# Queries and keys of the last batch, one row to a partition instead of eight, and the keys' block copy moved from ScalarE to VectorE

## The chip, the cores and the metric

The kernel runs on one core of one Trainium2 chip. Its time is the device time of one execution in microseconds, and the figure that counts is the median over runs. Before the change it is 291.07 us (8 runs, 290.84 to 291.77). A core has TensorE (PE in the profile; PEld is its weight load), VectorE (DVE), ScalarE (ACT), GpSimd (POOL, here Pool) and SyncE (SP), each with its own in-order instruction queue. All meet through semaphores. SyncE here only issues DMAs; Pool issues some too.

## What is computed

Chunked attention with a short context and eight memory keys, and behind it a mixing layer: two Fourier transforms, a normalisation and a two-layer network.

```python
B, H, S, D = 4, 8, 768, 64                 # batch, heads, rows, head width
for c in range(24):                        # chunks of 32 query rows
    # keys: 8 memory keys, then rows 32c-16 .. 32c+40 inside 0..768
    scores = q_c @ concat(mem_k, k_ctx).T / sqrt(D)
    out_c  = softmax(scores) @ concat(mem_v, v_ctx)
x = out.transpose(0, 2, 1, 3).reshape(B, S, 512)
u = x + real(fft(fft(x, axis=1), axis=2))
un = (u - mean(u)) / sqrt(var(u) + 1e-6)   # over the 512 columns
result = u + relu(un @ w_ch1) @ w_ch2      # 512 -> 2048 -> 512
```

## The kernel before, in words

**Attention.** Work goes by head pairs: `n` = 0 to 15, four pairs a batch, so the last batch (batch 3) has n = 12 to 15. A pair's two heads lie on partitions 0 to 63 and 64 to 127, head width down. Queries are needed as `qT` (128 x 768), keys as `kTb`: 12 blocks of 128 columns, block t serving 64 query rows. Columns 32 to 39 of a block hold the memory keys (`e_mkT`, VectorE), columns 40 to 127 the 88 context keys; neighbouring blocks overlap. Per pair there are two groups g of six blocks: `e_scores` makes 12 matmuls (six blocks, two heads) into the PSUM tile `sc`, `e_exp` takes the exponential on ScalarE (two instructions), `e_values` makes 24 matmuls into `xa` (`v` carries a column of ones that gives the sum), and `e_norm` divides on VectorE and writes into `xsb`. `sc` and `xa` exist once, `qT`, `kTb` and `kU` twice, `qs` and `ks` three times, `va` four times, the query transposes' target slot `qT` being freed by the second group's scores.

**How q and k become transposed.** For batches 0 to 2 (n < `TURNED * HP` = 12) a Pool DMA brings eight consecutive rows to each of 96 partitions (`e_load_qk`, L347), TensorE transposes them in 16 pieces (`turn`, L374), and ScalarE (VectorE in batch 0) copies them into natural order (`e_qT`, `e_kT`). For batch 3 Pool loads the same eight rows a partition, the two heads' columns side by side (L343, one DMA a head); a DMA transpose issued by SyncE turns them (`e_flip_q` L379, `e_flip_k` L382). Its result has the rows in the order (j, p), where row = 8p + j. `e_scores` (L431, L432) undoes that order for the queries by reading 8 runs of 8 and writing 8 x 8 scattered columns in PSUM, and `e_kT` (L410, ScalarE) for the keys, from the staging tile `kU` into `kTb`, 128 x 1056 elements. `kU` has zero margins for keys outside 0 to 767; Pool sets both `kU` tiles to zero at the start (L851).

**Mixing.** Per batch: row transforms (`zy`, `pq`, `ff` on VectorE, split in a high and a low half `hi`, `lo`, then PE matmuls `ps`), PSUM read out by ScalarE (`up`) and VectorE (`e_rest`), column transforms (PE, `pm`, into the PSUM banks `acc`, freed by VectorE's `e_sum` and `e_sum_back`), statistics, `un` on ScalarE, and the two network layers (`ph`, with ScalarE's `hT`, and `pc`, with VectorE's `osb`). For batches 1 to 3 SyncE's DMA transposes turn `un` into `unT` (L711).

**What sets the order.** A planner (`Plan`) gets every step with an engine, a cost, its predecessors and the slots that it takes and gives, runs a list schedule in planned time, and writes the instructions out in that order; the `ph` and `pc` blocks are fillers that it puts where PE would be idle. The order on every queue therefore depends on the planned costs. The steps of batch 3 are made in `attention` (L873 to L878): the two transposes as SP steps of 1.2 us that land 5 us later, the block copy as an ACT step of 2.05 us.

Of the kernel before, what the change touches and what calls it, by code (L numbers as in the profile page):

```python
# [11 lines left out]
BF16 = mybir.dt.bfloat16  # L12
# [5 lines left out]
LEFT = 16  # L18
RIGHT = 8
NMEM = 8  # L20
BIGM = 800.0
MEM0 = 32
# [9 lines left out]
def strided(src, off, dims):  # L32
    return bass.AP(tensor=src.tensor, offset=src.offset + off,
                   ap=[list(src.ap[0])] + [list(d) for d in dims])
# [143 lines left out]
def kernel(  # L178
# [11 lines left out]
    nc = tc.nc  # L190
    B, H, S, D = q.shape
    DM = out.shape[2]
    DFF = moe_w_ch1.shape[1]
    P = 128
    NST = S // P
    NDT = DM // P
    NHT = DFF // P
    NT = S // 64
    RB = 8
    QP = S // RB  # L200
    KP = QP + 4
    KOFF = LEFT // RB
# [8 lines left out]
    spool = ctx.enter_context(tc.tile_pool(name="stage", bufs=1))  # L211
    apool = ctx.enter_context(tc.tile_pool(name="attn", bufs=1))
# [20 lines left out]
        assert False  # L233

    NS = 3
    qs = [spool.tile([QP, 2, RB * D], BF16, name=f"qs{i}") for i in range(NS)]
    ks = [spool.tile([KP, 2, RB * D], BF16, name=f"ks{i}") for i in range(NS)]
    NV = 4
    va = [spool.tile([P, 2, NT, 66], FP32, name=f"va{i}") for i in range(NV)]
    NKT = 2  # L240
    KR, KS, NKU = 16, 128, 2
    kU = [spool.tile([P, RB, KS], BF16, name=f"kU{i}") for i in range(NKU)]
    kTb = [spool.tile([P, NT, P], BF16, name=f"kTb{i}") for i in range(NKT)]

    TURNED = 3
    cp_q = "p h j d -> p h (j d)"
    HP = H // 2
# [4 lines left out]
    add = plan.add  # L252
# [19 lines left out]
    ident_b = cpool.tile([P, P], BF16)  # L272
    turn_b = cpool.tile([KP, KP], BF16)
# [64 lines left out]
    def e_load_qk(n, i):  # L338
        b, pr = seq[n]
        src, dst = ((q, qs), (k, ks))[i]  # L340
        if b >= TURNED:
            for hh in range(2):
                nc.gpsimd.dma_start(  # L343
                    dst[n % NS][0:QP].rearrange("p h (j d) -> p (h j) d", d=D)[:, hh::2],
                    src[b, 2 * pr + hh].rearrange("(p j) d -> p j d", j=RB))
            return
        nc.gpsimd.dma_start(dst[n % NS][0:QP],  # L347
                            src[b, 2 * pr:2 * pr + 2].rearrange("h (p j) d -> p h (j d)", j=RB))
# [21 lines left out]
    def turn(out_, src, eye):  # L370
        w = eye.shape[1]
        for j in range(RB):
            for hh in range(2):
                nc.tensor.transpose(out_[64 * hh:64 * hh + 64, j * w:(j + 1) * w],  # L374
                                    src[:, hh, j * D:(j + 1) * D], eye)

    def e_flip_q(n):
        qT_of[n] = qT = apool.tile([P, RB, QP], BF16, tag="qT", bufs=2, name="qT")
        nc.sync.dma_start_transpose(qT, qs[n % NS].rearrange("p h c -> p (h c)"))  # L379

    def e_flip_k(n):
        nc.sync.dma_start_transpose(kU[n % NKU][:, :, KR:KR + QP],  # L382
                                    ks[n % NS][0:QP].rearrange("p h c -> p (h c)"))

    def e_turn_q(n):
        tr_of[n] = trq = aps.tile([P, S], BF16, tag="tr", bufs=1, name="trq")
        turn(trq, qs[n % NS], ident_b[0:QP, 0:QP])

    def e_qT(n):
        qT_of[n] = qT = apool.tile([P, S], BF16, tag="qT", bufs=2, name="qT")  # L390
# [3 lines left out]
    def e_turn_k(n):  # L394
        if n < HP:
            trk = bank("acc", [P, RB * KP], BF16, "trk")
        else:
            trk = aps.tile([P, RB * KP], BF16, tag="tr", bufs=1, name="trk")
        tr_of[n, 1] = trk
        turn(trk, ks[n % NS], turn_b)  # L400

    def e_mkT(n):
        b, pr = seq[n]
# [3 lines left out]

    def e_kT(n, eng=None):
        if n >= TURNED * HP:
            nc.scalar.copy(  # L410
                strided(kTb[n % NKT], MEM0 + NMEM, [[P, NT], [RB, 11], [1, RB]]),
                strided(kU[n % NKU], KR - KOFF, [[64 // RB, NT], [1, 11], [KS, RB]]))
            return
        trk = tr_of.pop((n, 1))
        (eng or nc.scalar.copy)(
            strided(kTb[n % NKT], MEM0 + NMEM, [[P, NT], [RB, 11], [1, RB]]),
            strided(trk, 0, [[64 // RB, NT], [1, 11], [KP, RB]]))
        if n < HP:
            let_go(trk)

    def e_scores(n, g):
        qT, kT = qT_of[n], kTb[n % NKT]
        sc_of[n, g] = sc = aps.tile([P, 2, 8, 64], FP32, tag="sc", bufs=1, name="sc")
        for t6 in range(6):
            t = 6 * g + t6
            for hh in range(2):
                r0 = 64 * hh
                if n < TURNED * HP:
                    own, to = qT[r0:r0 + 64, ts(t, 64)], sc[:, hh, t6, :]
                else:  # L430
                    own = strided(qT[r0:r0 + 64], t * 64 // RB, [[QP, RB], [1, 64 // RB]])  # L431
                    to = strided(sc[:, hh, t6, :], 0, [[1, RB], [RB, 64 // RB]])  # L432
                nc.tensor.matmul(to, kT[r0:r0 + 64, t, :], own, start=True, stop=True,  # L433
                                 tile_position=(r0, 0))

    def e_exp(n, g):
# [416 lines left out]
    def attention(n):  # L853
        nonlocal t_gate
        b, pr = seq[n]
        first = b == 0
        lq, lk = [add("POOL", 1.6 if b >= TURNED else 0.9, lambda i=i: e_load_qk(n, i),
                      take=(("qs", "ks")[i],), moved=3.1 if b >= TURNED else 1.2, grain=0.032 if b >= TURNED else 0.1, late=LATE if b else 0.0,
                      behind=t_gate if n == HP else t_xr[b - 2] if n == TURNED * HP else t_ck.get(n - 1),
                      rank={0: -4 + i, 1: -1.2 + 0.1 * i, 2: 10 + 0.1 * i}.get(n)) for i in range(2)]  # L860
        lv = add("SP", 2.5, lambda: e_load_v(n), [t_ones[n] if n < NV else None],
                 behind=t_x2.get(b - 2),
                 take=("va",), moved=2.6, grain=0.031, head=0.4, late=(0.0, 4.0, LATE, LATE)[b])
        t_lv[n] = lv
        t_ck[n] = lk
        if n == HP - 1:
            def e_gate():
                nc.gpsimd.tensor_copy(gate[64:65], va[n % NV][64:65, 1, NT - 1, 0:1])

            t_gate = add("POOL", 0.1, e_gate, [lv])  # L870
        mk = t_mk[n] = add("DVE", 0.2, lambda: e_mkT(n), [t_mkT, t_kTz[n % NKT], t_mk.get(n - 1)],
                           take=("kTb",))
        if b >= TURNED:  # L873
            eq = add("SP", 1.2, lambda: e_flip_q(n), [lq], take=("qT",), give=("qs",),
                     late=5.0, loose=True, behind=t_flip[0])
            t_flip[0] = tk = add("SP", 1.2, lambda: e_flip_k(n), [lk, t_uz], take=("kU",),
                                 give=("ks",), late=5.0, loose=True, behind=eq)
            ek = add("ACT", 2.05, lambda: e_kT(n), [tk, mk], give=("kU",))  # L878
        else:
            tq = add("PE", 0.40, lambda: e_turn_q(n), [lq, t_idb], take=("tr",), give=("qs",))  # L880
            dve = ("DVE", nc.vector.tensor_copy) if n < HP else ("ACT", None)
            eq = add("ACT", 0.80, lambda: e_qT(n), [tq], take=("qT",), give=("tr",),
                     rank=SINES - 0.5 if n == 0 else None)
            ktag = "acc" if first else "tr"
            tk = add("PE", 0.43, lambda: e_turn_k(n), [lk, t_idb, t_kz if n == 0 else t_kzs],
                     take=(ktag,), give=("ks",))
            ek = add(dve[0], 1.25 if dve[1] else 1.04, lambda: e_kT(n, dve[1]), [tk, mk],
                     give=(ktag,))
        for g in range(2):
            s_ = add("PE", 0.32, lambda g=g: e_scores(n, g), [eq, ek], take=("sc",),  # L890
                     give=("qT", "kTb") if g == 1 else ())
            t_sc[n, g] = s_
            t_exp[n, g] = x_ = add("ACT", 1.12, lambda g=g: e_exp(n, g),
                     [s_, t_masks, t_after.get(n)], take=("e1",), give=("sc",))
            tag = "mlp" if first and g == 1 else "xa"
            v_ = add("PE", 0.85, lambda g=g: e_values(n, g), [x_, lv, t_low[n % NV]], take=(tag,),
                     rank=len(plan.tasks) + (50 if (n, g) == (2, 1) else 25) if first else None,
                     give=("e1", "va") if g == 1 else ("e1",))
            take = ("xsb",) if g == 0 and n % HP == 0 else ()
            t_norm[n, g] = add("DVE", 0.78, lambda g=g: e_norm(n, g),  # L900
                               [v_, t_norm[n - n % HP, 0] if (n % HP, g) != (0, 0) else None],
                               take=take,
                               give=(tag,))
        return x_
# [284 lines left out]
```

The softmax here doesn't subtract the row's maximum and nothing guards it: scores larger than these inputs give would overflow.

## Time and profile before

| | before |
|---|---|
| median of 8 runs | 291.07 us |
| profiled execution | 291.56 us, of which span 289.9 us |
| granted TensorE clock over the span | 0.999 |
| PE busy | 273.2 us (94%) |
| ScalarE busy | 167.5 us (58%) |
| VectorE busy | 166.0 us (57%) |
| Pool busy | 65.2 us (22%) |
| PE busy, 127 to 172 us (batch 3's attention, batch 2's transforms) | 45.0 of 45 us |
| VectorE, ScalarE busy, 127 to 172 us | 32.1 and 30.5 us |
| PE, VectorE, ScalarE busy, 214 to 286 us (two-layer network alone) | 71.9, 9.3 and 24.7 of 72 us |

The page of a profile gives the busy time of each engine, the span in 40 slices (a digit is the busy share in tenths, 9 is 90% or more) and the clock in the same slices:

```profile
PE   1588989999999999999999999999999999999994
DVE  7866998862239876958675884985672012012011
ACT  5976545788777687846796466525660721712700
POOL 8853894330201083441001002010020000000000
PEclk9999999999999999999999999999999999999999
```

PE is close to full from the sixth slice on, and the clock is full throughout; slices 18 to 24 (123 to 174 us) are where batch 3's attention runs. Matmuls are pipelined, so a matmul's own duration (some 200 to 400 ns here) overlaps the next one; what a block costs is read from the chain of waits, which follows the work that ended last back from the end and puts blocks end to end. PE's busy digits therefore say only that it did not wait, not that it runs at its best.

### The profile page before, as it was taken

Reading aid. Unit: us, or ns where it says so; the run is one execution under the profiler, and the core shown is the slowest. Engines: PE = TensorE matmul, PEld = TensorE weight load, DVE = VectorE, ACT = ScalarE, POOL = GpSimd, SP = SyncE. Lnnn points to the kernel's source line nnn. Section 1 sums busy time; section 2 is a strip of 40 time slices with the busy share of each in tenths; the row PEclk is TensorE's granted clock in tenths of the full one; section 3 lists DMA queues with packets and bytes.
Section 4 is the critical chain, followed back from the end, with each engine's and each line's share of the span. In section 5 each row is a group of like instructions: output and inputs, shape, how many; then the busy total and the mean of one; then the engine's idle time right before and its main releaser. Section 6 shows DMA issues by size and latency. Waiting matters only on the chain.

```text
span 289.9 us, 7127 instructions
## 1 busy us (share of the span) xinstructions
PE 273.2 (94%) x2932; PEld 170.6 (59%) x2932; DVE 166.0 (57%) x345; ACT 167.5 (58%) x290; POOL 65.2 (22%) x115
## 2 busy tenths in 40 slices
PE   1588989999999999999999999999999999999994
PEld 1465678865665767556676656566654545545541
DVE  7866998862239876958675884985672012012011
ACT  5976545788777687846796466525660721712700
POOL 8853894330201083441001002010020000000000
PEclk9999999999999999999999999999999999999999
DMA  6999999999997999999997047675142504004204
GB/s 106 200 171 162 207 159 205 203 196 196 194 184 222 141 220 164 143 149 247 183 153 200 3 111 144 171 124 180 20 85 84 105 3 126 20 36 108 39 36 109
DMA packets 115968, 39.92 MB, mean 138 GB/s; under 512 B 104544, under 2 KB 111200, under 8 KB 115936
## 3 DMA queue, kind: packets, MB, share of 16 engines
q1 hardware_dynamic: 93744, 23.41, 44.2%
q0 software_dynamic: 21472, 15.21, 33.1%
q10 hardware_dynamic: 720, 0.85, 0.9%
q8 instruction: 23, 0.38, 0.6%
q14 instruction: 9, 0.07, 0.1%
HBM read 37.36 MB, written 13.37 MB: 175 GB/s over the span
## 4 chain that ended last, share of the span: by engine, by line
PE 86%; POOL 5%; DVE 4%; DMA 2%; issue 1%; POOLq 0%
PE pc L756 29%; PE ph L741 29%; PE xa L456 7%; PE ps L528 5%; PE pm L679 5%; PE sc L433 3%; DMA ks<-in_k_dram 2%; PE ps L668 2%; DVE ff L615 2%; PE trk L374 1%; PE trq L374 1%; POOL qs L347 1%; DVE hl L635 1%; DVE xsb L467 1%; PE pm L579 1%
## 5 line engine op out<-in xcount | busy, mean ns | idle before, releaser
L749 ACT ACTIVATE hT<-ph 128x384 f16<-128x384 f32 x128 | 61.9, 491 | 50.6 <-PE ph L741 49.8
L741 PE MATMUL ph<-unT,w_sb 128*128 128x384 f16 x512 | 88.1, 326 | 0.0
L756 PE MATMUL pc<-w_sb,hT 128*128 128x512 f16 x384 | 87.8, 380 | 0.0
L741 PEld LDWEIGHTS <-w_sb 128*128 128x128 f16 x512 | 48.6, 98 | 32.0 <-issue 0.4
L756 PEld LDWEIGHTS <-hT 128*128 128x128 f16 x384 | 35.9, 98 | 41.0 <-issue 0.4
L763 DVE SCALAR_TENSOR_TENSOR osb<-pc,rstd,xsb 128x512 f32<-128x512 f32 x24 | 18.0, 750 | 69.3 <-PE pc L756 64.8
L440 ACT ACTIVATE e<-sc,mbias 128x384 f32<-128x384 f32 x64 | 33.6, 577 | 19.2 <-PE sc L433 18.6
L456 PEld LDWEIGHTS xa<-va,e 128*64 128x64 f32 x672 | 21.9, 137 | 7.2 <-issue 6.2
L456 PE MATMUL xa<-va,e 128*64 128x65 f32 x672 | 25.8, 226 | 0.0
L699 ACT ACTIVATE un<-xsb,mu_s 128x512 f16<-128x512 f32 x24 | 16.9, 719 | 6.6 <-DVE mu_s L694 6.6
L540 ACT CAST up<-ps 128x386 f16<-128x386 f32 x16 | 9.6, 603 | 13.7 <-PE ps L528 11.6
L693 DVE BATCH_NORM_STATS2 st<-xsb 128x6 f32<-128x512 f32 x24 | 16.6, 691 | 0.7
L467 DVE TENSOR_TENSOR xsb<-xa,zs 128x384 f32<-128x384 f32 x28 | 15.6, 558 | 1.0
L466 DVE RECIPROCAL zs<-xa 128x6 f32<-128x6 f32 x28 | 5.3, 190 | 18.1 <-PE xa L456 17.7
L518 DVE TENSOR_TENSOR lo<-ff,hi 128x768 f16<-128x768 f32 x12 | 11.4, 953 | 4.7 <-ACT hi L513 4.7
L545 DVE TENSOR_TENSOR up<-ps,up 128x386 f16<-128x386 f32 x16 | 9.5, 597 | 6.9 <-ACT up L540 6.7
L433 PE MATMUL sc<-qT,kTb 64*128 64x64 bf16 x384 | 12.6, 205 | 0.5 <-ACT e L440 0.5
L374 PE MATMUL trq<-ident_b,qs 96*64 96x96 bf16 x192 | 7.0, 221 | 6.4 <-DMA qs<-in_q_dram 6.4
L433 PEld LDWEIGHTS <-kTb 64*128 64x128 bf16 x384 | 8.5, 100 | 7.3 <-issue 6.1
L513 ACT CAST hi<-ff 128x768 f16<-128x768 f32 x12 | 9.9, 827 | 3.3 <-DVE ff L505 3.0
L685 DVE TENSOR_TENSOR xsb<-pm,xsb 128x512 f32<-128x512 f32 x15 | 10.0, 672 | 3.2 <-PE pm L679 3.2
L571 POOL DMA_DIRECT2D xr<-x_back x3 | 2.3, 779 | 42.1 <-DMA x_back<-x_rows 42.1
(150 smaller groups left out, 356.7 us busy)
## 6 DMA issues: line engine op xcount, KB each, us to landing
va<-in_v_dram SPq DMA_DIRECT2D x32, 220.0 KB
w_sb<-in_moe_w_ch_dram POOLq DMA_DIRECT2D x8, 512.0 KB, 13.5
out_dram<-osb SPq DMA_DIRECT2D x12, 256.0 KB
qs<-in_q_dram POOLq DMA_DIRECT2D x12, 192.0 KB, 6.1
ks<-in_k_dram POOLq DMA_DIRECT2D x12, 192.0 KB, 6.7
x_rows<-xsb POOLq DMA_DIRECT2D x3, 768.0 KB, 5.6
xr<-x_back POOLq DMA_DIRECT2D x3, 768.0 KB, 5.6
out_rows<-osb SPq DMA_DIRECT2D x9, 256.0 KB
```

The lines of the kernel that those rows point to most:

```text
L433: nc.tensor.matmul(to, kT[r0:r0 + 64, t, :], own, start=True, stop=True, tile_position=(r0, 0))
L440: nc.scalar.activation(e1[:, :, :, ts(half, 32)], sc[:, :, 0:6, ts(half, 32)], AFT.Exp, bias=mbias[:, half:half + 1], scale=1.0 / math.sqr ...
L456: nc.tensor.matmul(xa[64 * half:64 * half + 64, st, hh, 0:65], e1[:, hh, t6, :], v1[:, hh, 6 * g + t6, 0:65], start=True, stop=True)
L467: nc.vector.tensor_tensor(xs[b][:, 3 * g:3 * g + 3, 2 * pr * D:(2 * pr + 2) * D] .rearrange("p s (h d) -> p s h d", h=2), xa[:, :, :, 0:D] ...
L528: nc.tensor.matmul(out_[:, sp, :], part[:, ab, sp * 3 + st, c0:c1], tab[:, sp, st, :], start=(st == 0 and i == 0), stop=(st == 2 and i == 1))
L679: nc.tensor.matmul(pm[:, par, :], lhs, rhs[:, par, :], start=(im == 0), stop=(im == 3))
L693: nc.vector.bn_stats(st6, xs[b][:, kt, :])
L699: nc.scalar.activation(un, xs[b][:, kt, :], AFT.Identity, bias=mu_of[b][:, kt, 0:1], scale=-1.0)
L741: nc.tensor.matmul(ph[:, 0:384], w1_sb[:, dt, ts(ht, P)], unT_of[b][:, dt, sh * 384:(sh + 1) * 384], start=(dt == 0), stop=(dt == NDT - 1))
L749: nc.scalar.activation(hT_of[b, sh][:, ht, :], ph[:, 0:384], AFT.Relu, bias=0.0, scale=-1.0)
L756: nc.tensor.matmul(pc_of[b, sh, stl], hT_of[b, sh][:, ht, ts(stl, P)], w2_sb[:, ht, :], start=(ht == 0), stop=(ht == NHT - 1))
L763: nc.vector.scalar_tensor_tensor(osb, pc, rstd_of[b][:, st:st + 1], xs[b][:, st, :], ALU.mult, ALU.add)
```

## The change

For batch 3 only, row 128a + p of a head now goes to partition p (a = 0 to 5), 128 partitions instead of 96, six rows each instead of eight. The DMA transposes, over 768 columns instead of 1024, then give queries and keys in natural order. `qT` is a plain 128 x 768 tile, `e_scores` has one form for all batches, `kU` becomes one run of 768 keys with margins of 16, and the copy into `kTb` reads and writes runs of 88 and is issued on VectorE with a planned cost of 0.6 us instead of 2.05 on ScalarE. `qs` and `ks` get 128 partitions; the older paths use the first 96 or 100 of them.

```diff
-    qs = [spool.tile([QP, 2, RB * D], BF16, name=f"qs{i}") for i in range(NS)]
-    ks = [spool.tile([KP, 2, RB * D], BF16, name=f"ks{i}") for i in range(NS)]
+    qs = [spool.tile([P, 2, RB * D], BF16, name=f"qs{i}") for i in range(NS)]
+    ks = [spool.tile([P, 2, RB * D], BF16, name=f"ks{i}") for i in range(NS)]
...
-    KR, KS, NKU = 16, 128, 2
-    kU = [spool.tile([P, RB, KS], BF16, name=f"kU{i}") for i in range(NKU)]
+    KR, NKU = 16, 2
+    kU = [spool.tile([P, KR + S + KR], BF16, name=f"kU{i}") for i in range(NKU)]
...
             for hh in range(2):
                 nc.gpsimd.dma_start(
-                    dst[n % NS][0:QP].rearrange("p h (j d) -> p (h j) d", d=D)[:, hh::2],
-                    src[b, 2 * pr + hh].rearrange("(p j) d -> p j d", j=RB))
+                    strided(dst[n % NS], hh * D, [[2 * D, NST], [1, D]]),
+                    src[b, 2 * pr + hh].rearrange("(a p) d -> p a d", p=P))
...
     def e_flip_q(n):
-        qT_of[n] = qT = apool.tile([P, RB, QP], BF16, tag="qT", bufs=2, name="qT")
-        nc.sync.dma_start_transpose(qT, qs[n % NS].rearrange("p h c -> p (h c)"))
+        qT_of[n] = qT = apool.tile([P, S], BF16, tag="qT", bufs=2, name="qT")
+        nc.sync.dma_start_transpose(qT.rearrange("p (a s) -> p a s", s=P),
+                                    qs[n % NS].rearrange("p h c -> p (h c)")[:, 0:S])
 
     def e_flip_k(n):
-        nc.sync.dma_start_transpose(kU[n % NKU][:, :, KR:KR + QP],
-                                    ks[n % NS][0:QP].rearrange("p h c -> p (h c)"))
+        nc.sync.dma_start_transpose(kU[n % NKU][:, KR:KR + S].rearrange("p (a s) -> p a s", s=P),
+                                    ks[n % NS].rearrange("p h c -> p (h c)")[:, 0:S])
...
         if n >= TURNED * HP:
-            nc.scalar.copy(
-                strided(kTb[n % NKT], MEM0 + NMEM, [[P, NT], [RB, 11], [1, RB]]),
-                strided(kU[n % NKU], KR - KOFF, [[64 // RB, NT], [1, 11], [KS, RB]]))
+            win = LEFT + 64 + RIGHT
+            nc.vector.tensor_copy(
+                strided(kTb[n % NKT], MEM0 + NMEM, [[P, NT], [1, win]]),
+                strided(kU[n % NKU], KR - LEFT, [[64, NT], [1, win]]))
             return
...
-                if n < TURNED * HP:
-                    own, to = qT[r0:r0 + 64, ts(t, 64)], sc[:, hh, t6, :]
-                else:
-                    own = strided(qT[r0:r0 + 64], t * 64 // RB, [[QP, RB], [1, 64 // RB]])
-                    to = strided(sc[:, hh, t6, :], 0, [[1, RB], [RB, 64 // RB]])
-                nc.tensor.matmul(to, kT[r0:r0 + 64, t, :], own, start=True, stop=True,
+                nc.tensor.matmul(sc[:, hh, t6, :], kT[r0:r0 + 64, t, :],
+                                 qT[r0:r0 + 64, ts(t, 64)], start=True, stop=True,
                                  tile_position=(r0, 0))
...
-            ek = add("ACT", 2.05, lambda: e_kT(n), [tk, mk], give=("kU",))
+            ek = add("DVE", 0.6, lambda: e_kT(n), [tk, mk], give=("kU",))
```

More of the change, by code (lines that the diff above doesn't have):

```diff
@@ L377, in e_flip_q @@
     def e_flip_q(n):
-        qT_of[n] = qT = apool.tile([P, RB, QP], BF16, tag="qT", bufs=2, name="qT")
-        nc.sync.dma_start_transpose(qT, qs[n % NS].rearrange("p h c -> p (h c)"))
+        qT_of[n] = qT = apool.tile([P, S], BF16, tag="qT", bufs=2, name="qT")
+        nc.sync.dma_start_transpose(qT.rearrange("p (a s) -> p a s", s=P),
+                                    qs[n % NS].rearrange("p h c -> p (h c)")[:, 0:S])
     def e_flip_k(n):
-        nc.sync.dma_start_transpose(kU[n % NKU][:, :, KR:KR + QP],
-                                    ks[n % NS][0:QP].rearrange("p h c -> p (h c)"))
+        nc.sync.dma_start_transpose(kU[n % NKU][:, KR:KR + S].rearrange("p (a s) -> p a s", s=P),
+                                    ks[n % NS].rearrange("p h c -> p (h c)")[:, 0:S])
     def e_turn_q(n):
         tr_of[n] = trq = aps.tile([P, S], BF16, tag="tr", bufs=1, name="trq")
-        turn(trq, qs[n % NS], ident_b[0:QP, 0:QP])
+        turn(trq, qs[n % NS][0:QP], ident_b[0:QP, 0:QP])
     def e_qT(n):
@@ L399, in e_turn_k @@
         tr_of[n, 1] = trk
-        turn(trk, ks[n % NS], turn_b)
+        turn(trk, ks[n % NS][0:KP], turn_b)
     def e_mkT(n):
```

## The prediction, made before the changed kernel ran

> **What bounds the kernel now.** I read the waits of TensorE (PE) first: what it waited for, us in total, times, longest.
>
> ```profile
> PE trq L374 <- DMA qs<-in_q_dram: 6.4, 3, 4.8
> ...
> PE trk L374 <- DMA ks<-in_k_dram: 1.2, 2, 0.8
> ...
> PE sc L433 <- ACT e L440: 0.5, 2, 0.3
> ```
>
> All its waits lie in the first 40 us; asked for 110 to 220 us alone the view lists none. So where the last batch's attention runs, the time is the sum of PE's own instructions, and other engines count only if PE comes to wait for them. The chain of waits (start, duration, what) prices these, back to back:
>
> ```profile
> 15.20 0.52 POOL kU L851
> 15.72 0.41 issue
> 16.14 0.95 POOL kU L851
> 17.09 0.58 POOL qs L347
> 17.68 5.96 DMA ks<-in_k_dram
> 23.68 0.55 PE trk L374 x16
> ...
> 121.44 0.28 PE sc L433 x12
> 121.72 4.42 PE pc L756 x20
> ...
> 129.67 1.83 PE pc L756 x8
> 131.50 0.85 PE xa L456 x24
> 132.36 0.44 PE sc L433 x12
> 132.80 2.06 PE ph L741 x12
> ...
> 169.69 1.73 PE pc L756 x8
> ```
>
> Two prices are to be seen. A block of 12 score matmuls costs 0.28 us in batch 2 (121.44) and 0.44 in batch 3 (132.36). And a large block costs 0.1 more after a score or value block (eight `pc` 1.83 after `xa`, 1.73 after `pm`; twelve `ph` 2.06 after scores against 1.95 elsewhere). The first lines show something else: Pool's two `kU` memsets stand ahead of the loads that PE waited for at 23.68.
>
> The rows of the tiles `kU`, `unT` and `sc` (min/median/max ns), then VectorE's copies by form (count, busy us, mean ns):
>
> ```profile
> L382 SPq DMA_TRANSPOSE kU<-ks x4: 1212/1316/2001, 121.6 to 153.8; - x4
> L410 ACT COPY kTb<-kU x4: 2026/2046/2071, 126.8 to 159.5; 128x1056 bf16<-128x1056 bf16 x4
> L711 SPq DMA_TRANSPOSE unT<-un x18: 1188/1214/1436, 116.4 to 215.7; - x18
> L433 PE MATMUL sc<-qT,kTb x144: 190/243/243, 110.4 to 168.5; 64*128 64x64 bf16 x144
> ```
>
> ```profile
> L415 DVE COPY kTb<-trk 128x1056 bf16<-128x1056 bf16 x4 | 5.0, 1254 | 1.7 <-PE trk L374 1.7
> L404 DVE COPY kTb<-mkT 128x96 bf16<-128x96 bf16 x16 | 3.6, 235 | 9.0 <-PE sc L433 8.9
> L553 DVE COPY dn<-up 128x768 f16<-128x768 f16 x4 | 1.4, 362 | 0.1
> ```
>
> **Part by part**
>
> *Scores.* Batch 3 has 4 head pairs (n = 12 to 15) of 2 blocks each. Plain runs are what batch 2 has, same shape: 8 x (0.44 - 0.28) = **-1.28 us**, all on PE.
>
> *Key copy.* ScalarE loses 4 x 2.05 = 8.2 us. PE waits for none of it, so this itself brings nothing. VectorE gains four copies, a form that the trace does not show. Nearest rows: 768 two-byte elements from SBUF take 362 ns, 96 take 178 to 191 when undisturbed, so 0.27 ns an element, and 1056 take **0.44 us**. Upper end 1.25, the row from PSUM. I take 0.44; VectorE is 71% busy from 127 to 172 us, and the four make 1.8 us of its 13 idle.
>
> *The planner's order.* The copy's planned cost falls from 2.05 to 0.6, and the planner lays out all queues anew. The changed program's instruction lists agree with the old up to the values of n = 11 (128.82). Then scores of n = 12 come 2.7 us earlier; those of 13 move behind `ph` and batch 2's even row transforms (`ps`), those of 14 and 15 behind its first column blocks (`pm`). From the last values on it is nearly the old order. PE does the same work, but it goes from a small block to a large one 17 times instead of 15: 2 x 0.1 = **+0.2 us**.
>
> Does PE now wait? I laid the old durations along the new lists from 129.67, each engine in order. The tight places:
> - Scores of 12, PE at 129.67. `kU` landed by 126.8 (ScalarE's copy starts there after waiting), VectorE ends the normalisation ahead of it at 127.83, the copy at 128.3 (129.1 at 1.25): spare 1.4 (0.6). Queued behind this copy is the next normalisation, whose values end only at 131.7.
> - Batch 2's first `ps`: PE 141.9, `lo` done 140.4. Its last `ps`: PE 153.2; `lo`, now behind the copy of 13, 151.5.
> - Third `pm` block: PE 162.8, its bank is read out at 162.1: spare **0.65**, the least.
> - Values of 14: PE 170.75. Their bank is freed by the normalisation of 13, which stands behind all six sums and statistics: 169.95, spare 0.8. The copy of 15 follows at 170.4, scores of 15 at 172.3.
>
> I cost the new order at no wait; each us by which a producer passes its spare is a us lost. On SyncE the transposes of 15 wait for the scores of 13 and go out near 155.5 instead of 152.4, covered until 170; batch 2's `un` transposes behind them are wanted near 187.
>
> *Transposes.* 96 x 1024 becomes 128 x 768: equal bytes. The issue takes 1.2 us at best for `kU` as for 128 x 512 `unT`: no change. Landing: the old key transpose of 12 took 5.2 us (121.56 to 126.8); 7 still fit. I take the old time.
>
> *Loads.* 768 pieces either way: 96 x 8 before, 128 x 6 now, 128 bytes at the destination. What grows shorter is the source's run, from 2048 bytes a partition to 256. The Trainium skill, DMA: Bandwidth & Descriptors, Specifications, speaks against this: under 512 bytes a transfer falls below line rate. The row for these loads is 3.5/7.6/9.3 us from issue to landing. If pieces count, nothing changes. If the rule means the source run and the time doubles, 15.2 us for the queries of 12 (second half issued at 102.65) end at 117.9, and their transpose, now at 114.28, slips 3.6 us with SyncE's queue behind it. Scores of 12 then wait 1.2 us. The old destination pieces are already below 512, so I take the row: 0.
>
> *Shared port.* The skill's SBUF - State Buffer, SBUF: two separate sides, lets a two-port VectorE copy and a Pool instruction exclude each other. Pool issues key loads from 127.34 to 128.95, over the copy of 12. By the rule the copy may end at 128.95 + 0.44 = 129.4, still before 129.67. The trace is mixed: a `mkT` copy took 0.98 us at 31.99 beside a Pool tensor operation, 0.18 at 124.88 beside another. Either way the sum holds.
>
> *Memset.* `kU` shrinks from 1024 to 800 elements. Pool's memset rows: 974 ns for 1024, 423 for 384, so 0.86 ns an element, 2 x 0.19 = 0.39 us earlier loads for n = 3. The end at full effect is -0.39. The other is 0: DMA is saturated there, and Pool's next work waits for values until 26.3. I take **-0.2**.
>
> **Sum:** -1.28 + 0.2 - 0.2 = -1.28, rounded -1.3. The profiled execution took 291.56 (span 289.9 and 1.66 around it): 290.3. It lies 0.5 above the median 291.07, so the median goes to **289.8**.
>
> **Rivals**
> - *B, the new order makes PE wait.* For: spares of 0.65 and 0.8 hang on a VectorE 71% busy, and the old order kept 1.3 at the same two places. Against: laid out with measured durations, none is passed. A wait of about 1 us: 290.8.
> - *C, late key transpose (slower).* Short source runs double the longest landing, 9.3, to 18.6: queries of 12 land at 121.3, their transpose slips 7 us, and the keys', fourth behind it on the same queue, lands at 133.8. Scores of 12, moved forward, wait until 134.3: 4.6 us, so 294.4. It turns the gain into a loss once the key transpose lands after 130.4. For: the skill's rule. Against: equal pieces, the 11.6 us of cover.
> - *E, the scattered order is not what makes scores slow,* so -1.28 goes and 291.1 stays. Against: 190 and 243 ns for one shape in one kernel.
>
> **Numbers.** Forecast 0.68, B 0.16, C 0.10, E 0.06. The forecast's own range is 289.4 (full memset gain, no extra 0.2) to 290.1 (none); with B, E and 0.2 of measurement it becomes 289.2 to 291.6, leaving out C and little more. No change means within 0.2%, 0.58 us, about what a measurement can tell. Faster: 0.66 from the forecast and 0.04 from B. Same: 0.02, 0.07 from B, 0.05 from E. Slower: 0.10 from C, 0.05 from B, 0.01 from E. So 0.70, 0.14, 0.16.
>
> **What would show it.** In the changed profile: score blocks of 0.28 in batch 3; `kTb` copies near 0.44 on VectorE; no PE wait after 110 us; transposes still at 1.2; PE's last values near 178.5 instead of 178.87; `trk` of n = 3 before 23.68. PE waiting for `kTb` near 129.7 would mean C, for VectorE at `pm` or `xa` between 160 and 175 B, scores at 0.44 E.

## The result, and the profile after

| | before | after |
|---|---|---|
| median, both measured in turn | 291.22 us (290.39 to 293.34, 53 runs) | **289.84 us** (289.22 to 291.7, 18 runs) |
| ratio after / before, 95% interval | | **0.9959** [0.9946, 0.9971] |
| profiled execution, span | 291.56, 289.9 us | 291.15, 289.4 us |
| ScalarE, VectorE busy, 127 to 172 us | 30.5 and 32.1 us | 25.1 and 35.8 us |

The ratio makes -1.19 us (-0.84 to -1.57); the medians alone lie 1.38 apart. So the change is faster, and the predicted 289.8 us is met. The profiled pair, though, differs by 0.4 us only, and that has to be explained. First the waits of TensorE (PE) in the changed kernel (what it waited for, us in total, times, longest), whole span:

```profile
PE trq L374 <- DMA qs<-in_q_dram: 6.6, 4, 4.6
PE mps L910 <- DVE mkb L904: 1.8, 1, 1.8
...
PE trk L374 <- DMA ks<-in_k_dram: 0.8, 2, 0.5
```

and the same view asked for 44 to 127 us alone:

```profile
PE trq L374 <- DMA qs<-in_q_dram: 1.2, 2, 0.7
```

The second answer is new: the kernel before waited for nothing after 40 us. From 127 us on PE waits for nothing here either. The chain of waits of the changed kernel (start, duration, what) says where the two late waits are and what followed:

```profile
15.15 0.52 POOL kU L849
15.67 0.18 issue
15.85 0.78 POOL kU L849
16.62 0.57 POOL qs L347
17.20 6.45 DMA ks<-in_k_dram
23.64 0.04 issue
23.69 0.54 PE trk L374 x16
...
54.54 18.81 DMA qs<-in_q_dram
73.34 0.04 issue
73.39 0.53 PE trq L374 x16
...
126.83 0.85 PE xa L454 x24
...
130.36 0.28 PE sc L430 x12
130.64 0.97 PE pc L754 x4
...
179.14 0.85 PE xa L454 x24
...
285.51 0.75 DVE osb L761
```

Three things are to be seen. First, both `kU` memsets are shorter and the loads of n = 3 go out at 17.20 instead of 17.68, yet `trk` starts at 23.69 instead of 23.68: the landing took 6.45 instead of 5.96. Second, batch 1's queries held PE at 73.39 (0.46 us, and 0.71 at 58.06). Third, the scores of batch 3 now cost 0.28 (130.36). The rows of the tiles `sc` (asked for 110 to 260 us, as before), `kU` and `kTb` (min/median/max ns) of the changed kernel:

```profile
L430 PE MATMUL sc<-qT,kTb x144: 190/190/200, 111.1 to 175.9; 64*128 64x64 bf16 x144
L383 SPq DMA_TRANSPOSE kU<-ks x4: 1209/1218/1372, 122.6 to 157.7; - x4
L412 DVE COPY kTb<-kU x4: 425/426/520, 128.4 to 170.5; 128x1056 bf16<-128x1056 bf16 x4
```

To compare kernels across executions I cut PE's chain at three points that exist in all of them: the first large `pm` block (near 47 us), the values of n = 10, second group (the `xa` block near 126 us; before has it at 126.14), and the last `osb` (before 285.89):

```profile
126.14 0.85 PE xa L456 x24
...
285.89 0.75 DVE osb L763
```

The **middle stretch** lies between the first two, the **late stretch** between the last two; batch 3's attention is in the late one. What each kernel is follows below.

| kernel | `pm` at | `xa` at | last `osb` at | middle | late |
|---|---|---|---|---|---|
| before | 47.79 | 126.14 | 285.89 | 78.35 | 159.75 |
| **after** | 47.16 | 126.83 | 285.51 | **79.67** | **158.68** |
| e1 memsets long | 47.05 | 125.41 | 284.09 | 78.36 | 158.68 |
| e2 margins only | 48.16 | 126.52 | 285.20 | 78.36 | 158.68 |
| e3 scattered write | 47.92 | 126.28 | 286.23 | 78.36 | 159.95 |
| e4 read in runs | 47.26 | 125.62 | 284.30 | 78.36 | 158.68 |
| e5 write and read | 48.10 | 126.45 | 286.41 | 78.35 | 159.96 |
| e6 copy on ScalarE | 47.04 | 125.40 | 283.86 | 78.36 | 158.46 |
| e7 longer statistics | 46.38 | 124.73 | 284.40 | 78.35 | 159.67 |
| e8 ten copies | 47.17 | 125.52 | 290.04 | 78.35 | 164.52 |
| e9 old layout, VectorE | 46.80 | 125.15 | 285.11 | 78.35 | 159.96 |
| e10 memsets twice | not in its chain | 126.14 | 284.82 | | 158.68 |
| e11 memsets behind | 47.03 | 125.39 | 284.06 | 78.36 | 158.67 |
| e12 both of e6 and e11 | 46.99 | 125.35 | 283.81 | 78.36 | 158.46 |

The late stretch is a figure of the kernel, not of the execution: e1, e2, e4, e10, e11 and the changed kernel, which have the same order and plain PSUM writes, agree to 0.01 us. The change took **1.07 us** out of it. The middle stretch is 78.35 or 78.36 in every other row that has it; the changed kernel's was 1.3 longer, 1.2 of it the two waits for queries. There the weights that are loaded ahead of them took 17.0 us (median) to land, against 13.5 in the profile before and 13.5 to 15.3 in the others; that these held the queries is not shown. So the last `osb` came 0.38 earlier than before: 1.07 gained late, 1.32 lost in the middle, 0.63 gained before 47 us, where the executions of this table differ by up to 1.8 us whatever was changed.

One likely cause of that spread is PE's own clock, which is not full throughout, as I had read it. The clock row of the profile prints full speed from the first slice on, but the clock records in the traces begin only at 16.4 us before and at 21.1 after, and until about then PE's blocks cost more: a score block took 0.43 us at 13.31 and 0.28 at 16.74 before, 0.43 at 18.85 and 0.28 at 21.88 after. In the other executions the first record stands at 15.9 (e11) to 23.0 us (e5). The three latest, e2 (21.6), e3 (22.4) and e5 (23.0), are also the three that reach `pm` last, at 47.92 to 48.16. Among the rest there is no such order, so the clock is at most one cause among others.

Four of the 18 runs took 291.15 us or more, the profiled one among them; the other fourteen lie between 289.22 and 290.42.

### The profile page after: what moved, and what is told of

It is laid out like the page before. It is cut to its first block, busy times and chain, and to the rows that moved or that the text cites. A ratio compares the mean times of both kernels' runs of the same rounds, so it can differ in the third digit from the quotient of the medians.

```text
span 289.4 us, 7131 instructions
## 1 busy us (share of the span) xinstructions
PE 273.6 (95%) x2932; PEld 171.2 (59%) x2932; DVE 167.7 (58%) x349; ACT 160.6 (55%) x286; POOL 65.5 (23%) x115
## 4 chain that ended last, share of the span: by engine, by line
PE 79%; DMA 9%; POOL 5%; DVE 4%; issue 1%; POOLq 0%
PE pc L754 29%; PE ph L739 26%; DMA qs<-in_q_dram 6%; PE xa L454 6%; PE ps L526 5%; PE pm L677 4%; PE sc L430 2%; DMA ks<-in_k_dram 2%; PE ps L666 2%; DVE ff L613 1%; PE trk L374 1%; PE trq L374 1%; POOL qs L347 1%; DVE hl L633 1%; DVE xsb L465 1%
## 5 line engine op out<-in xcount | busy, mean ns | idle before, releaser
L454 PEld LDWEIGHTS xa<-va,e 128*64 128x64 f32 x672 | 22.5, 141 | 7.9 <-issue 6.8
L454 PE MATMUL xa<-va,e 128*64 128x65 f32 x672 | 26.4, 229 | 0.0
L430 PEld LDWEIGHTS <-kTb 64*128 64x128 bf16 x384 | 7.7, 97 | 6.9 <-issue 5.5
L430 PE MATMUL sc<-qT,kTb 64*128 64x64 bf16 x384 | 11.6, 196 | 0.0
L392 ACT COPY qT<-trq 128x768 bf16<-128x768 bf16 x12 | 9.5, 795 | 3.5 <-PE trq L374 3.5
```

Of the source, the lines that this page charges most:

```text
L430: nc.tensor.matmul(sc[:, hh, t6, :], kT[r0:r0 + 64, t, :], qT[r0:r0 + 64, ts(t, 64)], start=True, stop=True, tile_position=(r0, 0))
L454: nc.tensor.matmul(xa[64 * half:64 * half + 64, st, hh, 0:65], e1[:, hh, t6, :], v1[:, hh, 6 * g + t6, 0:65], start=True, stop=True)
```

## The experiments

**The scattered scores: the write or the read?** Three kernels put the scatter back on the changed one's plain data. PE then takes other columns of queries, or puts the scores into another order.

```diff
 e3 (write):  to  = strided(to, 0, [[1, RB], [RB, 64 // RB]])          # n >= 12, PSUM
 e4 (read):   own = strided(qT[r0:r0 + 64], t * 64 // RB, [[QP, RB], [1, 64 // RB]])
 e5 (both)
```

> The changed kernel, with batch 3's score matmuls writing their 64 columns scattered into PSUM (8 x 8, as before the change) but reading plain runs; batch 3's query rows come out in another order within each 64. Theory: the scattered write in PSUM is what made a matmul 243 ns instead of 190, so the blocks of 12 cost 0.44 us again. Rival: the reading of runs of 8 did it, and the blocks stay at 0.28.

> The changed kernel, with batch 3's score matmuls reading queries in 8 runs of 8 elements, 96 elements apart (as before the change), and writing plain columns; batch 3 thus scores other query rows. Theory: 190 ns a matmul and 0.28 us a block, as reading runs of 16 bytes costs nothing. Rival: 243 ns and 0.44 us.

> The changed kernel, with batch 3's score matmuls in the old form on both sides (runs of 8 read, 8 x 8 scattered columns written); batch 3 scores other query rows. Both theories: 243 ns a matmul and 0.44 us a block, so PE's last block ends 1.28 us later than in the changed kernel relative to the values of n = 10.

The rows of `sc` in batch 3, asked for 126 to 185 us, first with the scattered write alone, then with the read in runs alone:

```profile
L433 PE MATMUL sc<-qT,kTb x96: 226/243/243, 129.7 to 176.6; 64*128 64x64 bf16 x96
```

```profile
L433 PE MATMUL sc<-qT,kTb x96: 190/190/200, 129.1 to 174.7; 64*128 64x64 bf16 x96
```

The write into 8 x 8 scattered columns takes all of the 53 ns a matmul and brings the late stretch to 159.95; the read of 8 runs of 8 elements (16 bytes) takes nothing, 158.68. Both together give 159.96. One run each: 291.91, 289.96 and 292.06 us, beside 291.7 of the kernel before. The whole of the prediction's first term is the PSUM write.

**The old engine for the copy, and so the old order.** The planned cost sets the order, so the copy on ScalarE at its old cost brings nearly the old lists back, with plain runs.

```diff
-            nc.vector.tensor_copy(
+            nc.scalar.copy(
...
-            ek = add("DVE", 0.6, lambda: e_kT(n), [tk, mk], give=("kU",))
+            ek = add("ACT", 2.05, lambda: e_kT(n), [tk, mk], give=("kU",))
```

> The changed kernel with the block copy of the keys back on ScalarE (plain runs of 88) at its old planned cost, so that the planner's order is close to the old one. Theory: PE does not wait for ScalarE here, the score blocks cost 0.28 us, and the two extra changes from small to large blocks (0.1 each) go: time about 0.2 us below the changed kernel, near 289.6. The ScalarE copy takes about 1.04 us as from PSUM, against 2.05 in the scattered form. Rival: moving the copy off ScalarE is part of the gain; then this kernel lies 0.5 us or more above the changed one.

Measured 289.64 us (289.07 to 290.42, 6 runs), ratio 0.9948 [0.9932, 0.9964]. The intervals overlap with the changed kernel's; the late stretch does not: 158.46 against 158.68. Old order and plain scores make -1.29 against before, so -1.28 was the scores alone, and the new order costs 0.22. In the late stretch of the traces PE goes from a score or value block to another kind of block 15 times before, in e6 and in e12, and 17 times in the changed kernel, e9 and e11, as the prediction counted. The copy itself, on ScalarE in plain runs:

```profile
L412 ACT COPY kTb<-kU x4: 1062/1076/1081, 125.2 to 157.8; 128x1056 bf16<-128x1056 bf16 x4
```

It takes about half as long as the one before (2046 ns), and PE does not wait for it.

**The new order with the old data.** The kernel before, with only the copy moved to VectorE and its planned cost at 0.6. As before, the copy writes runs of 88 but reads one element at a time, each 128 elements behind the last (the expectation's "runs of 8" is not what the code does).

```diff
-            nc.scalar.copy(
+            nc.vector.tensor_copy(
...
-            ek = add("ACT", 2.05, lambda: e_kT(n), [tk, mk], give=("kU",))
+            ek = add("DVE", 0.6, lambda: e_kT(n), [tk, mk], give=("kU",))
```

> The kernel before (eight rows to a partition, scattered scores), with only the key copy moved to VectorE at a planned cost of 0.6 us, so that it has the changed kernel's order. Theory: the score blocks cost 0.44 us, the new order costs two changes of block size, 0.2 us, and the stretch from the values of n = 10 to the last osb is 159.95 us (before: 159.75, changed: 158.68); the copy in runs of 8 takes up to 1.25 us, which still fits the spare of 1.4. Rival: moving the copy brings part of the gain, and the stretch falls below 159.5. The loads of eight rows a partition give a second look at their time to landing: near 7.6 us (the row-wise ones had medians of 6.6 to 8.7 in seven profiles).

```profile
L410 DVE COPY kTb<-kU x4: 1070/1078/1086, 126.7 to 169.8; 128x1056 bf16<-128x1056 bf16 x4
```

The row of `kTb` in this kernel shows copies of 1.08 us with the reads 128 elements apart, where plain ones take 0.43. PE does not wait for them either: the late stretch is 159.96, that is +0.21 against before, the order alone from the other side. One run: 290.82 us, against 290.89 of the kernel before beside it.

**The memsets.** First the old size, then only the margins set to zero:

```diff
 e1:  kU = [spool.tile([P, 1024], BF16, name=f"kU{i}") for i in range(NKU)]
 e2:  nc.gpsimd.memset(strided(kU[i], 0, [[KR + S, 2], [1, KR]]), 0.0)
```

> The changed kernel with kU tiles of 1024 elements again, so that Pool's two memsets are as long as before (974 ns each); all else as changed. Theory: the batch-3 part of the gain (-1.1 us) stays and the early part goes: the loads of n = 3 go out near 17.0 us as before, the first pm block starts near 47.8 us (changed kernel: 47.2), and the time is 0.2 to 0.6 us above the changed kernel, about 290.1 (ratio to before near 0.996). Rival: the shorter memset is worth nothing in the end, because what it wins is waited away later for batch 1's queries; then the time equals the changed kernel's within 0.2 us.

> The changed kernel with only the 2 x 16 margin elements of each kU set to zero, in one memset a tile (about 0.1 to 0.15 us each instead of 0.77). Theory: the loads of n = 3 go out 1.2 us earlier than in the changed kernel, PE's trk of n = 3 follows by up to 1 us, and the time falls by 0.3 to 1 us below the changed kernel (about 289.3). Rival: DMA is saturated and the values' loads on SyncE keep their time, so trk moves by less than 0.3 us and the time stays at 289.8; or batch 1's queries, loaded behind the weights, are waited for longer and nothing is left of it.

Measured: e1 290.21 us (289.57 to 291.42, 15 runs), ratio 0.9975 [0.9962, 0.9988]; e2 290.30 (289.62 to 290.86, 10 runs), ratio 0.9964 [0.9951, 0.9977]. e1's median lies 0.37 above the changed kernel's, as its theory had it; e2's lies 0.46 above, where its theory wanted a gain. The intervals overlap with the changed kernel's. In their profiles `xa` stands at 125.41 (long) and 126.52 (margins only), the wrong way round; but the clock records begin at 16.4 us in the first and at 21.6 in the second. This did not settle the term, so the memsets were moved by more than their own size: each done twice, then put behind the loads of n = 3 by their rank in the plan, then the latter with the copy on ScalarE.

```diff
 e10: [nc.gpsimd.memset(kU[i], 0.0) for _ in range(2) for i in range(NKU)], rank=20)
 e11: [nc.gpsimd.memset(kU[i], 0.0) for i in range(NKU)], rank=100)
 e12: as e11, with e6's two lines
```

> The changed kernel, but Pool sets each kU tile to zero twice in a row (four memsets instead of two): 2 x 0.77 = 1.55 us more on Pool ahead of the query and key loads of n = 3, nothing else moved. Theory T (Pool's time ahead of these loads passes on to PE, the -0.2 of the prediction being a part of 0.39): the loads go out near 18.75 instead of 17.2, trk of n = 3 starts near 24.9 to 25.2 instead of 22.7 to 23.7, and the median rises by 1.2 to 1.5, to near 291.2. Rival U (the loads land when the DMA engines have worked off what is queued, and what Pool's issue gains or loses up to about 1.5 us is gone on the way): trk within 22.7 to 23.9 as in the other executions, the median within 0.4 of 289.84.

> The changed kernel with the planner's rank of the kU memsets at 100 instead of 20. In the order of instructions this swaps one thing: the loads of n = 3 come first and the two memsets behind them; the tiles are wanted only near 116 us, and Pool idles 7.8 us after the loads, so the memsets cost nothing there. Theory T: the loads are issued 1.5 us earlier (near 15.7), trk of n = 3 starts between 21.5 and 22.5, and the median falls by 1.0 to 1.5, to near 288.6. Rival U: the landing grows by what the issue gains, trk stays between 22.5 and 23.7, the median within 0.4 of 289.84.

> The memsets behind the loads of n = 3 as in the run before, and the copy into kTb on ScalarE with its old planned cost of 2.05, so that the old order with its fewer changes from small to large blocks comes back: late stretch of PE 158.46 instead of 158.68, middle stretch 78.36. Theory T: 289.64 less 1.0 to 1.5, near 288.4. Rival U: within 0.4 of 289.64.

Pool in e10 from 14.9 us on (start, duration, what), by its timeline, and the chain of PE in the same execution:

```profile
15.09 2.88 POOL L849 MEMSET kU<- 128x800 bf16 x4
...
18.55 0.63 POOL L347 DMA_DIRECT2D ks<-in_k_dram  x1
```

```profile
17.06 0.43 PE sc L430 x12
...
21.80 0.28 PE sc L430 x12
22.08 0.85 PE xa L454 x24
22.93 0.34 PE trq L374 x16
23.27 0.36 PE trk L374 x16
```

The same two views of e11, from the key load on:

```profile
15.79 0.63 POOL L347 DMA_DIRECT2D ks<-in_k_dram  x1
16.46 1.48 POOL L849 MEMSET kU<- 128x800 bf16 x2
```

```profile
17.15 0.30 PE sc L430 x12
...
22.55 0.02 PE xa L454
...
22.87 0.03 PE trk L374
```

The two kernels issue the key load of n = 3 2.76 us apart (18.55 and 15.79), and PE reaches its `trk` 0.40 us apart (23.27 and 22.87), in both straight from its own earlier work, without a wait for these loads. Even the 0.40 need not be the memsets': the score block at 17 us took 0.43 in e10, whose clock records begin at 20.7 us, and 0.30 in e11, where they begin at 15.9. The medians are 290.27 us (290.0 to 291.19, 9 runs; ratio 0.9967 [0.9952, 0.9983]) and 289.89 (289.33 to 290.27, 6 runs; 0.9954 [0.9937, 0.997]); e12 gave 289.77 (6 runs; 0.9954 [0.9936, 0.9972]). Against the changed kernel's 289.84 e10 and e11 are +0.43 and +0.05 where theory T wanted +1.2 to +1.5 and -1.0 to -1.5, and their intervals overlap with its own. Measured in turn, the two lie 0.38 apart for their 2.76 us of issue, about a seventh, with intervals that overlap. Rival U holds for where PE arrives: most of what Pool's issue gains or loses here does not reach PE. Its mechanism is not shown as worded, since in these two PE's own earlier work decides, not the landing. e6 and e12 have the lowest medians, and no run tells them apart from the changed kernel by time.

**How large are the spares?** e7 makes VectorE do two of batch 2's statistics twice, ahead of a bank's read-out; e8 copies the keys of n = 12 ten times. One run each: 290.06 and 295.69 us, beside 290.89 of the kernel before.

```diff
 e7:  for _ in range(2 if b == 2 and kt < 2 else 1): nc.vector.bn_stats(...)
 e8:  for _ in range(10 if n == 12 else 1): nc.vector.tensor_copy(...)
```

> The changed kernel with batch 2's first two statistics instructions issued twice on VectorE (0.73 us more each), the planner's order unchanged. It tests the spares of the laid-out order at the third pm block and at the values of n = 14. Theory: the bank's read-out comes 1.46 us later and passes its spare of 0.65 to 0.7, so PE waits about 0.75 us before the third pm block, nothing more at the values of 14, and the stretch from the values of n = 10 to the last osb grows from 158.68 to about 159.4 us. Rival: the spares are larger than laid out, PE shows no wait and the stretch stays at 158.7.

> The changed kernel with the key copy of n = 12 made ten times on VectorE (same result), order unchanged. Theory: nine more copies at 0.34 us from start to start end 3.1 us later, which passes the spare of 1.4 at the scores of 12; PE waits there 1.5 to 1.8 us and the stretch from the values of n = 10 to the last osb grows from 158.68 to about 160.3 us. Rival: the scores of 12 are not held by this copy, and the stretch grows by less than 0.5 us.

The waits of PE from 112 to 184 us, in e7 and then in e8:

```profile
PE pm L677 <- DVE xsb L586: 0.8, 1, 0.8
```

```profile
PE sc L431 <- DVE kTb L413: 3.0, 1, 3.0
```

In e7 the spare of the third `pm` block was spent as laid out: wait 0.8 (expected 0.75), and the late stretch grew by 0.99, that wait and a first `pm` block of 1.05 instead of 0.87 behind it. In the changed kernel the bank is read out by 162.93 and PE arrives at 163.63: 0.70 of spare. e8 gave more than expected. The ten copies came 0.47 apart, each beginning only when the one before it had ended, so PE waited 3.0 us, not 1.5 to 1.8. But the late stretch grew by 5.84. The busy time of e8 by stretches (length, then PE, PEld, DVE, ACT and POOL busy with counts, granted clock, DMA share, GB/s):

```profile
129.00:131.00 2.00, 0.05 (x2) 0.00 (x0) 1.86 (x5) 0.00 (x0) 0.00 (x0) 1.00 1.78 116
131.00:133.00 2.00, 0.91 (x14) 0.55 (x15) 1.62 (x5) 0.31 (x1) 0.00 (x0) 0.62 1.24 175
133.00:135.00 2.00, 2.00 (x16) 0.89 (x16) 0.00 (x0) 0.74 (x2) 0.00 (x0) 0.50 1.40 155
...
137.00:139.00 2.00, 2.00 (x27) 1.01 (x25) 1.53 (x3) 0.50 (x2) 0.76 (x1) 0.68 0.98 221
139.00:141.00 2.00, 2.00 (x17) 1.20 (x14) 1.97 (x4) 0.95 (x2) 0.00 (x0) 1.00 1.05 377
```

The third number from the right is to be watched, the granted clock: 1.00, 0.62, 0.50, later 0.68 and 1.00 again. The 0.62 and 0.68 are means over a change: in slices of 0.2 us the clock is 1.00 until 131.4 and 0.50 from 131.6, and it is back at 1.00 from 138.4. The chain of e8 right behind the wait shows what that does to the blocks:

```profile
132.09 0.50 PE sc L431 x12
132.59 1.82 PE pc L755 x4
134.41 1.50 PE xa L455 x24
```

At full clock these take 0.28, 0.97 and 0.85. About half of what e8 lost (5.84 - 3.0) is PE at a lower clock after its idle time: from 132.09 on two score blocks, two `pc` and two value blocks took 7.0 us in place of 4.2.

## Why the prediction was right, point by point

- **Scores, -1.28.** Right: -1.29 in e6, with 0.28 for every block of batch 3. That the cause is the scatter, against rival E, is shown, and it is narrower than argued: the write alone (e3, e4).
- **Two more changes from small to large blocks, +0.2.** Right: +0.21 with the old scatter (e9), +0.22 with plain scores (158.68 - 158.46). Both together were predicted at -1.08 and measured at -1.07.
- **Key copy, 0.44 us on VectorE, no wait.** Right: 425 ns. ScalarE's freed time brought nothing, as said; e6 gives 4.3 us of it back and loses nothing.
- **Spares.** Scores of 12: the copy ends at 128.95 and PE comes at 130.36, 1.4 as laid out. Third `pm` block: 0.70 (0.65 laid out), shown as the edge by e7. Values of 14: 170.63 against 171.60, 0.97 (0.8). Rival B fell. Its mechanism is real (e7), but the place has to lose 0.7 us first.
- **Transposes and loads.** Issue 1.22 us, as taken. From issue to landing the row-wise loads (L343) took 8.5 us in the median here and 6.6 to 8.7 in e1 to e8, against 7.6 before and 6.9 in e9, which has the old pieces. The 512-byte rule of the Trainium skill (DMA: Bandwidth & Descriptors, Specifications), read for the source's run and with the doubling that the prediction assumed, would have made them 15.2; the measurement decides against that. Rival C fell.
- **Shared port.** The copy of 12 took 0.52 us here, 0.73 to 0.84 in e2, e3 and e4, and 0.42 in e1, each time beside Pool's key loads. So the step was right to keep both ends, and the spare of 1.4 hid the longest. What it did not see is that Pool can be the one that pays: in e5, e10 and e11 the copy took its 0.42 and Pool's issue grew (last section).
- **Memset, -0.2.** This is the term that was mis-sized, and its mechanism is not borne out: the memsets did shrink by 0.2 us each and the loads did go out 0.48 earlier, but no run shows it reach PE. The end named 0 fits the runs, and so does a small value within the uncertainty of the times. `trk` of n = 3 before 23.68 was the sign set for it, and it did not come. I had read the wait at 23.68 as one that Pool's issue sets. But in e10 the key load goes out 0.87 us later than before (18.55 against 17.68) and has landed when PE comes at 23.27: the landing took at most 4.7 us there, against 5.96 before and 6.45 after, so it is not the issue plus a fixed time.
- **PE's last values near 178.5.** Missed, 179.14, because this execution came to the values of n = 10 0.69 late (126.83 against 126.14); in e11, which has the same order, they stand at 177.70. From the values of n = 10 to these it is 52.31 us in both and was 52.73 before, so of the 1.07 only 0.42 is won by then and the rest behind them.

So the parts that were shown make -1.07, and the time fell by 1.19, with -1.07 inside its interval. That 289.8 was met to 0.04 us is partly luck: the working had 0.2 too much for the memsets, and this measurement's medians lie 0.3 further apart than the parts explain. The upper end of the forecast's own range is also 0.1 too high: without the memset term the working gives 290.0, not 290.1.

Open: what makes the landings in the first 24 us differ from one execution to the next, how much of the spread before 47 us is the clock's, and what held the weights and batch 1's queries in the profiled one. None of these was tried.

## What to carry to other kernels

Where PE is full, price PE's own blocks from the chain: here the only gain that was shown is a plain write into PSUM, and the freed ScalarE gave nothing. A planned cost that is changed moves the order of all queues, so count the dearer neighbours it makes and lay out every producer's spare, not only the moved instruction's. A wait in a stretch where DMA lands in varying time, and where PE's clock rises at a different time in each execution, is a poor base for a gain: move the issue by more than the gain before you believe in it.

## What was not expected of the hardware

- An idle PE can cost more than its wait: 3.0 us of idle cost 5.84, since the granted clock stood at 0.5 for 6.8 us; 0.8 us of idle (e7) left it at 1.00 and cost 0.99. The Trainium skill (TensorE: Matmul & The Clock Gate, Part 1) has half the clock after an idle window of about 3.4 us. The length agrees with the traces: in their clock records every stretch at full clock lasts a whole number of 3.413 us, 273.07 (80) before and 112.64 (33) and 157.01 (46) in e8, and so does the half one of e8, 6.83 (2). But the clock of e8 fell at 131.47, when PE had been idle for 2.4 us: the 3.41 us before began at 128.06, and PE was busy until 129.05. So the window need not be idle throughout.
- Writing its 64 columns into PSUM in steps of 8 costs a score matmul 53 ns; reading its queries in 8 runs of 8 costs nothing.
- A copy of 1056 elements takes 0.43 us on VectorE when it reads runs of 88, and 1.08 when it reads elements 128 apart; on ScalarE 1.08 and 2.05.
- VectorE's copy and Pool's issue of a DMA can hold each other up, one or the other. In the changed kernel, e2, e3, e4 and e8 the copy of 12, begun within Pool's second issue, ended 0.26 us after it and took 0.52 to 0.84 us. In e5, e10 and e11 it took 0.42 there, and that issue took 1.04 to 1.09 us instead of 0.82. In e1 and e7 the copy began near the end of the first issue, and neither shows a wait. What decides who pays is open. The copy and Pool's two issues, by the timelines of e4 and then of e10:

```profile
127.22 0.84 DVE L412 COPY kTb<-kU 128x1056 bf16<-128x1056 bf16 x1
126.07 1.73 POOL L343 DMA_DIRECT2D ks<-in_k_dram  x2 [0.52 <-DMA kU<-ks]
```

```profile
127.74 0.42 DVE L412 COPY kTb<-kU 128x1056 bf16<-128x1056 bf16 x1
126.62 1.95 POOL L343 DMA_DIRECT2D ks<-in_k_dram  x2 [0.55 <-DMA kU<-ks]
```
